# Head pairs recorded five units apart in place of four, with a new table of offsets

## Chip, core and metric

The kernel runs on one core of a Trainium2 chip. The metric is the device time of one execution in microseconds (us); the kernel before takes 849.22 us, the median of three runs (847.69 to 849.58). Engines are called PE (TensorE), DVE (VectorE), ACT (ScalarE), POOL (GpSimd) and SP (SyncE, which issues the DMAs).

## The reference, cut to what matters

Attention over 4 batches and 8 heads of 576 tokens, followed by two networks of two layers each, 512 to 2048 to 512, on 2304 tokens. The attention is the sum of one on means of four tokens and one in which a token sees its neighbours less than four away.

```python
q_d = q.reshape(B, H, Sd, 4, D).mean(axis=3)            # the same for k, v
out_up = np.repeat(sm_attn(q_d, k_d, v_d), 4, axis=2)
scores = np.where(np.abs(pos[:, None] - pos[None, :]) < 4, scale * q @ k.T, -1e9)
out_local = softmax(scores) @ v
x = (out_up + out_local) as 2304 x 512
h = x @ w_in                                            # first network
x = (np.maximum(h, 0.0) + np.log1p(np.exp(-np.abs(h)))) @ w_out
h = x @ w2_in                                           # second network
return (h * np.cos(h)) @ w2_out
```

## The kernel before, in words

Attention is done for a pair of heads at a time: 16 pairs, four to a batch, named p00 to p33 (batch, then pair). The networks go over five tiles of tokens (four of 512, one of 256). A layer's 2048 features are 16 units f of 128. In the names of the operations "L1 t f" is unit f of tile t in the first layer of the first network (matmuls "mm", then abs, relu, exp, ln, and G, gh, gl, which make the float16 parts of the result), "L2 t f d" its second layer (d is a half of the outputs), "L2 t f mm, keep, plus, turns, sin" the first layer of the second network and "L4 t f d" its last. Layer one of tile 0 takes float32 matmuls for its first six units (L1279 on PE; L1288, L1292 and L1296 on ACT; L1300 on DVE, which empties the PSUM buffer h) and float16 ones for the others (L1343, with L1440 to L1452 on ACT and L493 on DVE); the second layer is L1316 (float32) or L1524 (float16); the second network is L1378 and L1574. The four big weights (w1i, w1o, w2i, w2o) arrive compressed in eight blocks each. A block is loaded into one of two staging buffers stg, rebased on ACT (L638), joined on DVE (join1 L482, join2 L646), bounded on ACT (L668), and after a maximum over all partitions (PE L523 "wmax spread", DVE L529 "wmax", two small DVE steps "wfit") split into a high and a low half (L497, L493).

A pair's steps, by letter: A are the scores of the neighbour attention (PE L813, L819), A4 their exponential (ACT L854), B those of the pooled one (PE L912, L919; B1a and B2 are ACT L934 and L939, three instructions), C turns the weights round (PE L974; copies C0 and C1, ACT L503), D the same for the pooled ones (PE L1010, L994; copy D1, ACT L503), E is the product with the values (PE L1080, L1099; output E1, DVE L1123).

A planner sets the order. Each operation has a cost and one engine, or a choice of two (some copies and scalings go to ACT or DVE, whichever is free). A backward pass gives each a due time, on PE in the order in which the operations were recorded. Then `MOVES` adds offsets to these by name ("p13" for a whole pair, "p13 D1#1" for the first operation of that name). A list scheduler takes the operations by due time, puts each engine's instructions in one fixed order, and gives out the buffers: two PSUM buffers h for the first layers during the attention stage (four from about 130 us on), four larger ones ("any"). Where PE would stand idle for long in the first part of the program, the scheduler puts in a zero matmul (L1865, "filler"). So one changed offset can change the order on all engines, and the order of loads on SP.

`POS1`, `POS2` and `POS3` say after how many recorded units of the first network the pairs p10 to p13, p20 to p23 and p30 to p33 are recorded; p00 to p03 stand at the start. On the chip each engine works through its fixed order and waits at semaphores.

Of the kernel before, what the change touches and what calls it, by code (L numbers as in the profile page):

```python
# [23 lines left out]
B, H, S, D = 4, 8, 576, 64  # L24
# [26 lines left out]
POS2 = (37, 41, 45, 49)  # L51
POS3 = (54, 58, 62, 66)
# [355 lines left out]
def build(tc, qk, vw, vd, mask, w1i, w1o, w2i, w2o, out):  # L408
# [3 lines left out]
    with ExitStack() as ctx:  # L412
# [1208 lines left out]
        back = [(1, 0, f) for f in range(F0, NF)]  # L1621
        pos = dict(zip([*POS1, *POS2, *POS3], pairs[4:]))
        at = 0
# [326 lines left out]
```

## Time and profile before

| | |
|---|---|
| runs | 847.69, 849.22, 849.58 us |
| the profiled execution | 849.41 us, of which 847.3 us are the span of its trace |
| PE busy | 98% of the span |
| DVE busy | 85%; 96% from 48 to 100 us |
| ACT busy | 63%; 80% from 48 to 100 us |
| granted TensorE clock | 1.00 in all slices |
| data moved | 59.6 MB, mostly in the first 100 us |

The profile is one execution. A timeline row gives the start and the length of a run of like instructions, "xN" how many, and in brackets the idle time ahead of it with what ended that. PE's ends are modelled and overlap the next start by some tenths, so the distance from start to start is the better length: the 18 matmuls 128x512 in float16 that start at 214.03 us stand 0.22 us apart.

### The profile page before, as it was taken

How to read it: one execution, taken by the hardware profiler on the slowest of the kernel's cores; microseconds unless marked ns; L12 is line 12 of the kernel's file. 1: busy time of each engine (PE TensorE's matmuls, PEld its weight loads, DVE VectorE, ACT ScalarE, POOL GpSimd, SP SyncE). 2: the span in 40 equal slices, each digit the busy share in tenths (PEclk: the TensorE clock that was granted, in tenths of full speed). 3: DMA queues.
4: the chain of work that ended last, by engine and by line, in shares of the span. 5: the costliest groups of instructions: out<-in, count | busy, mean ns of one | idle time of the engine just before them, and what ended most of it. 6: DMA issues, size and time to landing. Idle time of an engine off the chain costs nothing.

```text
span 847.3 us, 15779 instructions
## 1 busy us (share of the span) xinstructions
PE 832.5 (98%) x6342; PEld 493.3 (58%) x6342; DVE 718.0 (85%) x1483; ACT 530.4 (63%) x960; POOL 1.8 (0%) x9
## 2 busy tenths in 40 slices
PE   7999999999999999999999999999999999999998
PEld 3654454555545555444557876666657667567564
DVE  6999999988668865999999989988699889678763
ACT  3568899686356567599989965544265655435431
POOL 0000000000000000000000000000000000000000
PEclk9999999999999999999999999999999999999999
DMA  9888440102210300205214200000000100000010
GB/s 276 274 291 298 164 159 27 59 6 90 62 45 1 117 1 2 67 36 196 100 50 150 101 1 1 1 1 27 26 1 1 51 1 1 24 27 1 1 50 25
DMA packets 14504, 59.57 MB, mean 70 GB/s; under 512 B 1696, under 2 KB 2080, under 8 KB 10336
## 3 DMA queue, kind: packets, MB, share of 16 engines
q1 hardware_dynamic: 14432, 58.58, 20.3%
q8 instruction: 49, 0.80, 0.4%
q14 instruction: 23, 0.19, 0.1%
HBM read 53.85 MB, written 4.72 MB: 69 GB/s over the span
## 4 chain that ended last, share of the span: by engine, by line
PE 83%; DVE 9%; DMA 4%; ACT 3%; issue 1%; POOL 0%; POOLq 0%; DVEq 0%; SPq 0%
PE any L1574 22%; PE any L1524 20%; PE h L1378 19%; PE h L1343 18%; DMA vd<-vd 2%; DMA stg<-w1i 2%; DMA stg<-w1o 1%; PE any L1099 1%; DVE w1i_t L646 1%; DVE sm L485 1%; DVE w1o_t L646 1%; DVE w1i_t L493 1%; PE any L819 1%; DVE vd L485 1%; PE any L974 1%
## 5 line engine op out<-in xcount | busy, mean ns | idle before, releaser
L1574 PE MATMUL any<-w1i_t,g 128*128 128x512 f16 x864 | 198.9, 379 | 1.0 <-DVE w1o_t L499 0.8
L1343 PE MATMUL h<-xt,w1i_t 128*128 128x512 f16 (+1 forms) x888 | 178.0, 356 | 0.1
L1378 PEld LDWEIGHTS <-w2i_t 128*128 128x128 f16 x1536 | 150.3, 98 | 33.8 <-issue 0.9
L1524 PE MATMUL any<-g,w1o_t 128*128 128x512 f16 (+1 forms) x792 | 158.1, 353 | 0.0
L1574 PEld LDWEIGHTS <-g 128*128 128x128 f16 x864 | 84.5, 98 | 87.8 <-issue 1.9
L1343 PEld LDWEIGHTS <-w1i_t 128*128 128x128 f16 x888 | 86.4, 98 | 83.7 <-issue 2.1
L1524 PEld LDWEIGHTS <-w1o_t 128*128 128x128 f16 x888 | 85.5, 98 | 79.4 <-issue 1.2
L485 DVE TENSOR_TENSOR g<-td,g 128x512 f16<-128x512 f32 (+1 forms) x146 | 92.0, 630 | 5.6 <-ACT g L503 2.4
L1378 PE MATMUL h<-xt,w2i_t 128*128 128x256 f16 x720 | 94.8, 273 | 0.7 <-ACT pu L1406 0.7
L1476 ACT ACTIVATE tc<-ta 128x512 f32<-128x512 f32 (+1 forms) x80 | 46.6, 585 | 58.0 <-DVE ta L485 47.9
L1378 PE MATMUL h<-w1o_t,w2i_t 128*128 128x256 f16 x624 | 79.4, 273 | 0.0
L1465 ACT ACTIVATE ta<-hs,quarter,i 128x512 f32<-128x512 f32 x64 | 51.5, 809 | 41.0 <-DVE hs L485 39.0
L503 ACT ACTIVATE g<-td 128x512 f16<-128x512 f32 (+1 forms) x78 | 46.2, 592 | 40.8 <-DVE td L1480 33.0
L1440 ACT ACTIVATE ta<-h,i 128x512 f32<-128x512 f32 (+1 forms) x74 | 47.0, 635 | 24.4 <-PE h L1343 23.5
L485 DVE TENSOR_TENSOR hs<-h,hs 128x512 f32<-128x512 f32 (+1 forms) x96 | 56.5, 598 | 6.3 <-PE h L1378 5.9
L1480 DVE SCALAR_TENSOR_TENSOR td<-hs,r,tc 128x512 f32<-128x512 f32 x64 | 48.0, 749 | 13.3 <-ACT tc L1476 11.8
L1444 ACT ACTIVATE tb<-h,r 128x512 f32<-128x512 f32 (+1 forms) x74 | 47.0, 635 | 15.5 <-PE h L1343 15.5
L493 DVE SCALAR_TENSOR_TENSOR td<-ta,sg,tb 128x512 f32<-128x512 f32 (+1 forms) x64 | 43.8, 684 | 13.2 <-ACT ta L1452 12.5
L485 DVE TENSOR_TENSOR ta<-ta,tb 128x512 f32<-128x512 f32 (+1 forms) x80 | 50.5, 636 | 1.3
L1452 ACT ACTIVATE ta<-ta,one 128x512 f32<-128x512 f32 (+1 forms) x74 | 49.9, 676 | 1.4
L1470 DVE TENSOR_SCALAR tb<-ta 128x512 f32<-128x512 f32 (+1 forms) x80 | 31.6, 398 | 14.8 <-ACT ta L1465 14.5
L1448 ACT ACTIVATE ta<-ta 128x512 f32<-128x512 f32 (+1 forms) x74 | 43.0, 583 | 0.2
(197 smaller groups left out, 1044.5 us busy)
## 6 DMA issues: line engine op xcount, KB each, us to landing
qk<-qk SPq DMA_DIRECT2D x16, 589.0 KB, 7.9
stg<-w1i SPq DMA_DIRECT2D x8, 1024.0 KB, 6.4
stg<-w1o SPq DMA_DIRECT2D x8, 1024.0 KB, 5.0
stg<-w2i SPq DMA_DIRECT2D x8, 1024.0 KB, 6.3
stg<-w2o SPq DMA_DIRECT2D x8, 1024.0 KB, 4.8
vw<-vw SPq DMA_DIRECT2D x16, 320.0 KB, 4.0
out<-w1o_t SPq DMA_DIRECT2D x17, 256.0 KB, 2.0
vd<-vd SPq DMA_DIRECT2D x8, 288.0 KB
```

The lines of the kernel that those rows point to most:

```text
L485: eng[e].tensor_tensor(out=out, in0=in0, in1=in1, op=op)
L493: nc.vector.scalar_tensor_tensor(out=out, in0=raw, scalar=s, in1=other, op0=ALU.mult, op1=op)
L1343: nc.tensor.matmul(h.t[:, 0:n], l, r, start=(i == 0), stop=(i == 11))
L1378: nc.tensor.matmul(h.t[:, a : a + 256], l, r, start=(i == 0), stop=(i == n - 1))
L1440: act(n, 1, True), lambda: nc.scalar.activation(out=a(), in_=h.t[:, 0:n], func=AF.Abs, scale=col(o.i1, f)),
L1444: act(n, 1, True), lambda: nc.scalar.activation(out=b(), in_=h.t[:, 0:n], func=AF.Relu, scale=col(o.r1, f)),
L1452: act(n, 1), lambda: nc.scalar.activation(out=a(), in_=a(), func=AF.Ln, bias=one),
L1465: act(n, 2, psum), lambda: nc.scalar.activation(out=a(), in_=h.t[:, a0 : a0 + n], func=AF.Identity, scale=col(o.i2, f), bias=quarter), [h, ...
L1476: act(n), lambda: nc.scalar.activation(out=r(), in_=a(), func=AF.Sin, scale=TWOPI),
L1480: dve(n, False, 1), lambda: nc.vector.scalar_tensor_tensor(out=td.t[:, 0:n], in0=h.t[:, a0 : a0 + n], scalar=col(o.r1, f), in1=r(), op0=AL ...
L1524: nc.tensor.matmul(a.t[:, i, 0:n], l, r, start=(first and j == 0), stop=(last and j == 2))
L1574: nc.tensor.matmul(a.t[:, i], l, r, start=(f == 0 and j == 0), stop=(f == NF - 1 and j == 2))
```

## The change

The pairs p20 to p33 are recorded five units apart where they were four apart, with p20 one unit later (38 for 37) and p33 seven (73 for 66). The `MOVES` table is another: of its entries nearly all are replaced. Nothing else differs, so what is computed by which matmul is the same. From `before` to `after` the lines of the code move by 11 (L1279 becomes L1290). One filler more is put in (77 for 76), and eight copies or scalings go from ACT to DVE.

```diff
-POS2 = (37, 41, 45, 49)
-POS3 = (54, 58, 62, 66)
+POS2 = (38,43,48,53)
+POS3 = (58,63,68,73)
 MOVES = {
...
-    "L1 0 15": 28.5, "L1 0 15 ln#1": -68, "L1 0 2 abs#1": 262, "L1 0 3": -132, "L1 0 4": -424.5, "L1 0 5": 18.5,
...
+    "L1 0 15": 129, "L1 0 15 mm#1": -13, "L1 0 2": -130.5, "L1 0 4": 48, "L1 0 5": 18.5, "L1 0 6": -45,
...
```

The new table moves instructions from the first microsecond on. Three places follow, each first in the kernel before and then in the changed one.

PE, about 60 us into the program, the first layer's third and fourth unit of tile 0. h_829 and h_830 (h_814 and h_813 after) are the two PSUM buffers, raw_161 to raw_164 the four parts of the input. Before:

```order
L1279 MATMUL h_829<-raw_161,w1i_t 128x512
L1279 MATMUL h_829<-raw_162,w1i_t 128x512
L1279 MATMUL h_829<-raw_163,w1i_t 128x512
L1279 MATMUL h_829<-raw_164,w1i_t 128x512
L912 MATMUL any_89<-qd_119 64x144 x4
L919 MATMUL any_89<-qd_119 32x144 x4
L1279 MATMUL h_830<-raw_161,w1i_t 128x512
L1279 MATMUL h_830<-raw_162,w1i_t 128x512
```

After:

```order
L923 MATMUL any_85<-qd_120 64x144 x4
L930 MATMUL any_85<-qd_120 32x144 x4
L1290 MATMUL h_814<-raw_161,w1i_t 128x512
L1290 MATMUL h_814<-raw_162,w1i_t 128x512
L1290 MATMUL h_814<-raw_163,w1i_t 128x512
L1290 MATMUL h_814<-raw_164,w1i_t 128x512
L1290 MATMUL h_813<-raw_161,w1i_t 128x512
L1290 MATMUL h_813<-raw_162,w1i_t 128x512
```

Before, the scores B of pair p12 stand between the two units (L1 0 4 and L1 0 3); after, the two units (L1 0 5 and L1 0 4) follow each other directly, and the pair's step that stood between them has gone elsewhere.

ACT at the same place, from the ln of unit L1 0 0 to the ln of unit L1 0 1 (ta_94 and ta_95 are the two units' work buffers). Before:

```order
L1296 ACTIVATE ta_94<-ta_94,one 128x512
L638 ACTIVATE w1i_t<-stg_108 128x1024
L668 ACTIVATE w1i_t,bd_w1i<-w1i_t 128x1024
L934 ACTIVATE nd_235<-nd_235 128x3
L497 ACTIVATE up_133<-any_85 128x144
L939 ACTIVATE ed_128,rs_231<-any_89,nd_235 128x144 x3
L1292 ACTIVATE ta_95<-ta_95 128x512
L1296 ACTIVATE ta_95<-ta_95,one 128x512
```

After:

```order
L1307 ACTIVATE ta_94<-ta_94,one 128x512
L1299 ACTIVATE ta_95<-h_813 128x512
L865 ACTIVATE sm_126<-sm_126 128x640
L679 ACTIVATE w1i_t,bd_w1i<-w1i_t 128x1024
L945 ACTIVATE nd_235<-nd_235 128x3
L1303 ACTIVATE ta_95<-ta_95 128x512
L950 ACTIVATE ed_128,rs_231<-any_85,nd_235 128x144 x3
L649 ACTIVATE w1i_t<-stg_109 128x1024
L1307 ACTIVATE ta_95<-ta_95,one 128x512
```

The abs of unit L1 0 1 (L1299) and the exponential of pair p11's scores (L865) now stand between the two logarithms; up (L497) does not.

DVE at the end of the first network, about 482 us into the program, at the maximum of the last two blocks of w2o (L529 on red_261, L540 after). td_98 holds a unit's result, L505 and L485 (L516 and L496 after) make its two float16 parts. Before:

```order
L529 TENSOR_REDUCE red_267<-h_829 128x1
L529 TENSOR_REDUCE red_261<-h_3491 128x2
L493 SCALAR_TENSOR_TENSOR td_98<-ta_94,sg_216,tb_96 128x256
L482 TENSOR_SCALAR s_w2o<-red_261 128x4
L482 TENSOR_SCALAR sx_199<-red_267 128x1
L482 TENSOR_SCALAR s_w2o<-s_w2o 128x4
L529 TENSOR_REDUCE red_269<-h_830 128x1
```

After:

```order
L504 SCALAR_TENSOR_TENSOR td_98<-ta_94,sg_216,tb_96 128x256
L540 TENSOR_REDUCE red_261<-h_3430 128x2
L493 TENSOR_SCALAR c_1_183<-sx_187 128x1
L493 TENSOR_SCALAR s_w2o<-red_261 128x4
L516 CAST g_101<-td_98 128x256
L493 TENSOR_SCALAR s_w2o<-s_w2o 128x4
L496 TENSOR_TENSOR g_101<-td_98,g_101 128x256
```

Before, the maximum stands ahead of the result of unit L1 4 14, which PE takes up four products (L2 4 12 and 13, two halves each) after the spread; after, it stands between the result of unit L1 4 13 and its two float16 parts, and PE takes up that unit (L2 4 13 0) as the next thing after the spread.

## Rows read from the trace of the kernel before

**Rows 1.** The page: busy time and share of the span, instructions by engine.

```profile
PE 832.5 (98%) x6342; PEld 493.3 (58%) x6342; DVE 718.0 (85%) x1483; ACT 530.4 (63%) x960; POOL 1.8 (0%) x9
```

**Rows 2.** Windows: stretch, us, busy time (and instructions) by engine, granted clock, DMA share, GB/s.

```profile
48.00:100.00 52.00, 49.80 (x375) 24.41 (x375) 49.94 (x102) 41.78 (x83) 0.00 (x0) 1.00 0.74 256
100.00:128.00 28.00, 27.89 (x209) 14.24 (x208) 27.72 (x57) 27.73 (x48) 0.00 (x0) 1.00 0.49 163
128.00:215.00 87.00, 87.00 (x715) 43.68 (x714) 79.83 (x164) 67.18 (x121) 0.00 (x0) 1.00 0.16 49
476.00:482.00 6.00, 6.00 (x57) 5.18 (x56) 6.00 (x11) 5.94 (x14) 0.00 (x0) 1.00 0.00 0
```

**Rows 3.** Timeline of PE, 57 to 71 us.

```profile
57.60 0.38 PE L1865 MATMUL any<-zero 128*128 128x512 f16 x1 [0.30 <-ACT aTd L503]
...
60.53 3.70 PE L1279 MATMUL h<-raw,w1i_t 128*128 128x512 f32 x8 [0.29 <-DVE g L1300]
...
65.47 3.70 PE L1279 MATMUL h<-raw,w1i_t 128*128 128x512 f32 x8 [0.45 <-DVE g L1300]
69.75 1.55 PE L1279 MATMUL h<-raw,w1i_t 128*128 128x512 f32 x3 [0.58 <-DVE g L1300]
```

**Rows 4.** Timeline of PE at 86 us.

```profile
86.11 0.38 PE L523 MATMUL h<-ident_s,bd_w1i 128*128 128x128 bf16 x4 [0.38 <-DVE g L1300]
```

**Rows 5.** ACT's groups, 40 to 130 us: count, busy us and mean ns, idle before.

```profile
L638 ACT ACTIVATE w1i_t<-stg 128x1024 f32<-128x1024 f32 x6 | 7.0, 1166 | 4.6 <-DMA stg<-w1i 4.6
L668 ACT ACTIVATE w1i_t<-w1i_t 128x1024 bf16<-128x1024 f32 x8 | 8.6, 1080 | 4.6 <-DVE w1i_t L646 4.6
L1440 ACT ACTIVATE ta<-h,i 128x512 f32<-128x512 f32 x7 | 4.8, 690 | 1.1 <-PE h L1343 0.8 <-DVE td L493 0.2
L939 ACT ACTIVATE ed<-any,nd 128x144 f32<-128x144 f32 x12 | 4.4, 385 | 0.0
L1296 ACT ACTIVATE ta<-ta,one 128x512 f32<-128x512 f32 x6 | 4.3, 723 | 0.1
L1292 ACT ACTIVATE ta<-ta 128x512 f32<-128x512 f32 x6 | 3.8, 632 | 0.0
L1288 ACT ACTIVATE ta<-h 128x512 f32<-128x512 f32 x6 | 3.6, 600 | 0.0
L503 ACT ACTIVATE aTd<-any 72x576 f32<-72x576 f32 x5 | 3.3, 652 | 0.0
L854 ACT ACTIVATE sm<-sm 128x640 f32<-128x640 f32 x4 | 2.9, 757 | 0.0
```

**Rows 6.** Timeline of DVE, 47 to 49 us.

```profile
47.84 0.82 DVE L857 TENSOR_REDUCE rs<-sm 128x10 f32<-128x640 f32 x1 [0.83 <-ACT sm L854]
```

**Rows 7.** Timeline of PE, 214 to 219 us.

```profile
214.03 4.05 PE L1524 MATMUL any<-g,w1o_t 128*128 128x512 f16 x18
218.65 0.58 PE L994 MATMUL any<-ident,ed 128*128 128x128 f32 x3 [0.57 <-DVE sm L485]
```

**Rows 8.** Timeline of all engines at the second network's start, 494 to 498 us.

```profile
495.50 1.28 ACT L1476 ACT_TABLE_LOAD   x1
...
497.74 0.82 PE L1378 MATMUL h<-xt,w2i_t 128*128 128x256 f16 x6 [0.72 <-ACT pu L1406]
```

**Rows 9.** DVE's groups, 462 to 482 us, columns as in rows 5.

```profile
L485 DVE TENSOR_TENSOR g<-td,g 128x256 f16<-128x256 f32 x6 | 2.5, 422 | 0.1
L529 DVE TENSOR_REDUCE red<-h 128x2 f32<-128x256 f32 x3 | 1.3, 420 | 0.0
L505 DVE CAST g<-td 128x256 f16<-128x256 f32 x3 | 0.9, 293 | 0.1
```

**Rows 10.** Timeline of PE at the last change of tile, 812 to 816 us.

```profile
812.86 2.75 PE L1574 MATMUL any<-w1i_t,g 128*128 128x512 f16 x12
815.88 0.81 PE L1574 MATMUL any<-w1i_t,g 128*128 128x512 f16 x3 [0.27 <-DVE w1o_t L499]
```

**Rows 11.** Timeline of PE, the first microseconds.

```profile
2.06 3.60 PE L1865 MATMUL any<-zero 128*128 128x512 f16 x9 [2.06 <-POOL zero L1854]
```

139 rows, old and new, of the table MOVES are left out of this document.

## The prediction

> **What bounds the kernel now.** I read the page first: PE is busy for 98% of the span [rows 1], and from 128 to 215 us it is busy without a gap while DVE and ACT are not [rows 2]. So the time is what PE has to do plus the places where PE waits, and a change that leaves the matmuls as they are can only move those places. I read the windows next, to see what paces the early part: from 48 to 100 us DVE is busy 49.94 of 52 us and PE 49.80 with all waits and fillers in it, and from 100 to 128 us ACT is busy 27.73 of 28 [rows 2]. There PE waits for results of engines that are themselves full. Last I read PE's timeline for the waits one by one, taking lengths from start to start, since ends are modelled. A float32 unit of layer one (8 records of L1279) lasts about 3.6 us when nothing stops it (3.70 in the row, the ends overlapping); the one at 65.47 is followed by the next at 69.75, that is 4.28, of which some 0.65 are the wait for G [rows 3]. Counted so, PE loses 3.5 us between 55 and 95 us: at 57.60, 60.53, 65.47 and 69.75 [rows 3], at 86.11 and just ahead of it [rows 4], and in two of less than 0.2. Behind 100 us it loses little: 0.73 at 218.65, where the D of pair p22 waits for DVE (18 matmuls of 0.22 from 214.03 end at about 217.9) [rows 7]; 0.88 at 497.74, where a PSUM buffer of the second network is emptied late because ACT loads a table for 1.28 us at 495.50 [rows 8]; and 0.41 to 0.43 at each of four changes of tile in the last layer, as at 815.88, which starts 3.02 us after 12 matmuls of 0.216 each began [rows 10]. These 6.8 us (3.5 + 0.73 + 0.88 + 4 x 0.42) and the first 50 us are all that an order can win; nothing sets a floor under what it can lose.
>
> **The change part by part.** All sums go against the profiled execution, 849.41 us, of which the trace spans 847.3; it is 0.2 us above the median of the runs. The loads, weights and matmuls are the same, so no term comes from work, apart from one filler more: +0.22, the step of a matmul of its size [rows 7].
>
> *Units 0 to 5 of tile 0 (about 50 to 70 us).* Layer one of this stage has two PSUM buffers. A unit's matmuls start when the unit two places before has been emptied by G on DVE, and G needs ln on ACT. In the new order L1 0 4 follows L1 0 5 directly, and between the G's that free their buffers ACT has, from ln to ln, abs 0.60, the exponential of p11's scores 0.76, a bound 1.08, B1a 0.21, exp 0.63, three B2 of 0.385, a rebase 1.17 and ln 0.72 [rows 5], 6.3 us by the means and about 5.4 when neighbours overlap by a tenth each. DVE's twelve instructions in the same place come to 4.9. PE has one unit of 3.6 [rows 3]. PE waits the difference: 1.3 by DVE, 2.7 by ACT without overlap, and I take 1.8. Ahead of it L1 0 5 waits for the first G: DVE has 17 instructions since p10's B, 9.3 us by their groups' means, PE 8.5 us of matmuls, and with the way between engines 1.1 (0.6 to 1.5). Behind it p10's D waits for the copy C1, which on ACT stands behind the abs of L1 0 4: 0.60 and two copies of about 0.5 and 0.4, against p10's C and one spread, 0.65 on PE; with the way there and back 0.9 (0.5 to 1.2). The units L1 0 6 and L1 0 8 then cost 0.4 (0 to 0.8). Together 4.2.
>
> *The last early pair (to about 95 us).* PE's p13 E needs the copy D1 on ACT. In the new order ACT has 23 instructions from the relu of L1 0 13 to that copy, of 0.50 to 1.17 each, 18.0 us by their means [rows 5]; PE has two float16 units of 12 matmuls of 0.22, six half-units of the float32 second layer of some 1.75, p13's C and D and a spread, 17.0 up to E. ACT is full there already in the kernel before [rows 2]. I take 0.8 (0 to 1.5; the upper end if the load of w1o's block 5, whose rebase is among the 23, comes late too).
>
> So the early stage loses 5.0 in place of 3.5: **+1.5**, between -1.1 with all lower ends and +4.2 with all upper ones. The cover of these waits is gone where the pair's step between two units has gone; before, p12's B stood there and the wait behind it was still 0.45 [rows 3].
>
> *128 to 460 us.* The wait at 218.65 goes, since p22's D has other work ahead of it: -0.73 [rows 7]. p22's A and E and p32's E now stand nearer to what they wait for (a bank that DVE empties against 1.7 us of PE's work): +0.6 (0 to 1.8), as DVE has free time here [rows 2]. Sum **-0.13**. What is late next is PE itself.
>
> *The change to the second network (470 to 500 us).* The new order goes past the table load with other matmuls in between: -0.88 [rows 8]. In its place PE has the spread of the last two blocks of w2o directly ahead of L2 4 13, and on DVE the maximum stands ahead of that unit's float16 parts. From the end of the spread PE waits for the maximum 0.42, one or two small steps of 0.15, the cast 0.29 [rows 9] and the way there and back, some 0.4: about 1.4, and a little more where the low part (0.42) follows late; I take 1.5. Below it is 0.6, if DVE reads the spread while PE still has matmuls of L2 4 12. Above it is 3.5, since the spread itself needs the bound of w2o's block 6, which now stands behind another rebase, a high half and a bound of more than 1 us each on an ACT that is busy 5.94 of 6 us here [rows 2]. L4 0 0 0 then waits for the low part of L2 0 0: +0.5 (0 to 1.3, one table load). Sum **+1.1**.
>
> *Changes of tile in the last layer (560 to 820 us).* Before, four of them have some 1.3 us of matmuls between the last use of a bank and its next, and wait 0.42; the order after has so little at two only (L4 1 0 1 and L4 4 0 0), and 1.95 or more at the others: **-0.85** [rows 10].
>
> Sum: 0.22 + 1.5 - 0.13 + 1.1 - 0.85 = +1.8, and 849.4 + 1.8 is **851.3 us**.
>
> *The clock.* PE's granted clock is 1.00 in every stretch here [rows 2], also behind the waits of rows 3. [...]
>
> **The rivals.** *The early waits only change place.* DVE and ACT have the same work before p13's E as before and are full [rows 2]; if they set the pace, PE gets to the end of that stage at the same time wherever it waits, and the +1.5 is 0. For it: 49.94 of 52 us on DVE. Against it: PE's waits come from order inside a few us, and DVE's share falls when it waits in turn. With 1.0 to 1.5 at the spread the sum is then -0.2 to +0.3, about 849.5.
>
> *Faster.* DVE waits for the exponential of p10's scores for 0.83 at 47.84 [rows 6], just ahead of the first G. In the new order other work stands there. If DVE and ACT come 1.1 us or more earlier to the G of L1 0 0, then L1 0 5 no longer waits, and the gain passes on to L1 0 4, L1 0 6 and p13's E, all of which wait for these two engines; of 5.0 only p10's D with 0.9 stays. Early stage -2.6, total 849.4 + 0.22 - 2.6 - 0.13 + 1.1 - 0.85 = 847.2. It decides from about 1.1 us on, and 0.83 is short of that; so it is the lesser case.
>
> [...]
>
> *The spread waits for the bound.* The term of 1.5 is then 3.5 and with the upper ends of two others the time is about 855. For it: ACT has next to no free time at 476 to 482 us [rows 2].
>
> **How the numbers follow.** Chances: the sum as it stands 0.50, early waits that only change place 0.27, faster 0.13, the bound 0.06, the clock 0.04. Of the first, whose own spread is about 849.9 to 853.5, I count 0.44 as slower by over 0.2% and 0.06 within it; of the second 0.25 within and 0.02 faster; the third is faster, the last two slower. 0.2% is 1.7 us, about what a measurement of this kernel can tell from no change: slower means above 850.9, faster below 847.5. So slower 0.54, same 0.31, faster 0.15. The range goes from 848.0, which leaves out most of the faster case, to 855.0, which takes in the bound's case.
>
> **What the profile after would show.** PE idle for over 1 us ahead of L1 0 5 and L1 0 4 with G as the releaser; p10's D with ACT's copy; the spread of w2o followed by an idle time of 1.2 to 1.8 us ahead of L1535, released by DVE; no wait at p22's D; two waits at changes of tile in place of four. The prediction is wrong if PE comes to p13's E no later than before against its own work (then the second or the third case holds), if the maximum of w2o hides, or if a wait shows that I saw no cause for, such as a load that comes late because the loads' order on SP is another.

## The result, and the profile after

The changed kernel takes 853.77 us (four runs, 853.31 to 854.21), the kernel before 848.46 (four runs, 846.03 to 849.58): the ratio is 1.0068, with a 95% interval from 1.0047 to 1.0089. That is slower by more than 0.2%. Its profiled execution took 854.17 us and spans 852.3, before 849.41 and 847.3: 5.0 us more in the span where the prediction's sum had 1.8. The direction and the range held; the size did not.

The page's busy times after, which answer to [rows 1]:

```profile
PE 837.2 (98%) x6343; PEld 494.9 (58%) x6343; DVE 721.1 (85%) x1491; ACT 521.9 (61%) x952; POOL 1.8 (0%) x9
```

PE does one matmul more (the filler). Its busy time is 4.7 us longer all the same, and slower matmuls are one reason: the windows after, with columns as in [rows 2], show a stretch at a lower clock.

```profile
48.00:100.00 52.00, 47.23 (x364) 23.54 (x364) 46.40 (x96) 43.93 (x85) 0.00 (x0) 0.93 0.58 190
56.00:60.00 4.00, 1.15 (x17) 0.44 (x17) 2.85 (x5) 4.00 (x7) 0.00 (x0) 0.83 0.90 264
60.00:64.00 4.00, 4.00 (x5) 1.82 (x6) 4.00 (x11) 4.00 (x12) 0.00 (x0) 0.50 0.98 314
64.00:68.00 4.00, 4.00 (x9) 1.65 (x8) 2.73 (x5) 1.76 (x4) 0.00 (x0) 0.81 0.34 135
100.00:128.00 28.00, 27.72 (x164) 13.31 (x162) 28.00 (x50) 27.55 (x52) 0.00 (x0) 1.00 0.68 240
```

From 48 to 100 us PE is busy 2.57 us less than before and DVE 3.54 less, and the granted clock, 1.00 before, is 0.93, with 0.50 from 60 to 64 us. From 100 to 128 us PE's busy time is within 0.2 us of that before.

To see where the 5.0 us went, I followed PE's steps in order and took from the start of each the sum of all PE work ahead of it, every kind with its own step from start to start. What is left is the time that PE has lost by then:

| PE has lost, us | before | after | difference | predicted |
|---|---|---|---|---|
| up to 48 us | 7.05 | 5.79 | -1.3 | none |
| from there to p13's E (123.72 before, 130.66 after) | 4.45 | 10.05 | +5.6 | +1.5 |
| from there to 460 us | 2.73 | 2.48 | -0.25 | -0.13 |
| change to the second network | 1.07 | 2.50 | +1.4 | +1.1 |
| from there to the end | 1.87 | 1.14 | -0.73 | -0.85 |
| one filler more | | | +0.22 | +0.22 |

The rows add up to the 5.0 us. The terms behind p13's E came out within 0.3 us of the prediction. The early stage alone cost +4.3 (-1.3 and +5.6) where I had +1.5. Its first row need not come from the order: in nine traces of the change and of kernels made from it by later edits, whose instructions are the same up to there, the first matmul of layer one starts between 44.97 us (e7_more) and 47.67 us (e6_end2), in the change at 45.27. So single traces are best compared from that matmul on. The timeline of all engines after shows how it begins, at the place of [rows 3]:

```profile
56.00 1.12 ACT L649 ACTIVATE w1i_t<-stg 128x1024 f32<-128x1024 f32 x1 [2.90 <-DMA stg<-w1i]
...
57.15 0.69 DVE L493 TENSOR_SCALAR w1i_t<-w1i_t 128x1024 int32<-128x1024 int32 x1 [3.12 <-ACT w1i_t L649]
57.76 0.42 DVE L496 TENSOR_TENSOR sm<-any,nm 128x256 f32<-128x256 f32 x1
...
58.05 0.71 ACT L1307 ACTIVATE ta<-ta,one 128x512 f32<-128x512 f32 x1
...
58.23 0.48 PE L923 MATMUL any<-qd 64*64 64x144 f32 x8 [2.82 <-DVE sm L496]
```

Block 5 of w1i is loaded from 47.45 us, when its staging buffer comes free, and lands at 55.98. ACT has its rebase (L649) next in its order and stands still 2.90 us for it; the ln of L1 0 0 (L1307) is queued behind. DVE has the block's join1 (L493) next and stands still 3.12 us; the second half of p11's A3 (L496) is queued behind that, and PE's B of p11 needs it. All three engines wait for one load. PE's part of the sequel, up to L1 0 2 (75.58 us after, 69.75 before):

```profile
59.97 9.86 PE L1290 MATMUL h<-raw,w1i_t 128*128 128x512 f32 x16 [0.62 <-DVE g L1311]
69.66 0.71 PE L985 MATMUL any<-ident,sm 128*128 128x128 f32 x5
...
71.22 0.85 PE L1021 MATMUL any<-ident,ed 128*72 128x128 f32 x6 [0.80 <-ACT aT L514]
72.06 0.59 PE L1876 MATMUL h<-zero 128*128 128x512 f16 x2
73.05 0.40 PE L534 MATMUL h<-ident_s,bd_w1i 128*128 128x128 bf16 x4 [0.40 <-ACT w1i_t L679]
73.58 0.59 PE L1876 MATMUL any<-zero 128*128 128x512 f16 x2
```

L1 0 5 and L1 0 4 stand in the first row. No idle time shows between them, yet the sixteen matmuls last 9.7 us, to the start of the next row, in place of 7.2: L1 0 5 ran at a granted clock of 0.56 on average (0.50 up to 64 us) and took 6.26 us in place of 3.6. PE is not seen waiting for the G of L1 0 1 there, since it is slow instead of idle: that G ends at 64.97, 1.4 us behind the point where a unit at 1.00 would have ended (59.97 and 3.6), and L1 0 4 starts at 66.23, so 1.26 us of the slow unit came through. The next G on DVE then stands still 1.51 us for the ln of the slow unit:

```profile
64.28 0.69 DVE L1311 SCALAR_TENSOR_TENSOR g<-h,ta 128x512 f32<-128x512 f32 x1 [0.23 <-ACT ta L1307]
...
68.47 0.69 DVE L1311 SCALAR_TENSOR_TENSOR g<-h,ta 128x512 f32<-128x512 f32 x1 [1.51 <-ACT ta L1307]
```

DVE's share is the key to what follows. The windows from zero to the start of L1 0 2, before and after; PE has done 60.2 and 60.7 us of work by then, so the two points compare:

```profile
0.00:69.75 69.75, 61.98 (x843) 35.39 (x844) 60.31 (x117) 38.46 (x96) 1.77 (x9) 1.00 0.86 283
```

```profile
0.00:75.58 75.58, 67.22 (x879) 37.65 (x879) 63.56 (x124) 42.99 (x102) 1.77 (x9) 0.95 0.80 268
```

PE comes there 5.83 us later. DVE was busy 3.25 us more ahead of that point (63.56 and 60.31), and not busy 2.58 more (12.02 and 9.44). Of the 2.58, 0.35 are a longer wait for the first load (2.34 in place of 2.00) and 2.23 are what is left of the waits for block 5 (3.12) and behind the slow unit (1.51), less smaller waits that went. In three more traces with the same early order (e4_end, r_after, e6_end2) the 12.02 are 10.74, 11.26 and 13.48. The 3.25 are other work that the new table puts ahead of L1 0 2. By the durations of single instructions they are the two joins of one more block of w1i, 1.90; two more maxima and four of the small steps behind them, 1.64; a G, 0.69; steps for the scale of the next tile, 0.73; against them p10's output E1 and one A3 moved behind, -1.6. That the two differences add up to the 5.83 is so by construction; whether PE follows DVE here is what the experiments had to show.

Late in the program the timeline of PE after shows what stands in place of [rows 8] and [rows 10]:

```profile
486.62 0.29 PE L534 MATMUL h<-ident_s,bd_w2o 128*128 128x128 bf16 x2
487.87 0.27 PE L1535 MATMUL any<-g,w1o_t 128*128 128x256 f16 x1 [0.97 <-DVE g L516]
488.33 1.36 PE L1535 MATMUL any<-g,w1o_t 128*128 128x256 f16 x11 [0.19 <-DVE g L496]
...
598.37 1.46 PE L1585 MATMUL any<-w1i_t,g 128*128 128x512 f16 x6 [0.25 <-DVE w1o_t L510]
...
819.58 0.81 PE L1585 MATMUL any<-w1i_t,g 128*128 128x512 f16 x3 [0.27 <-DVE w1o_t L510]
```

Directly behind the spread of w2o PE waits for the float16 parts of L1 4 13, the cast (L516) first and the low part (L496) after it: 1.15 and 0.35 from start to start, and 0.44 ahead and behind. The wait for the table load has gone. Two changes of tile wait in place of four.

### The profile page after: what moved, and what is told of

Read it like the earlier page. It is cut to its first block, busy times and chain, and to the rows that moved or that the text cites. A ratio compares the mean times of both kernels' runs of the same rounds, so it can differ in the third digit from the quotient of the medians.

```text
span 852.3 us, 15790 instructions
## 1 busy us (share of the span) xinstructions
PE 837.2 (98%) x6343; PEld 494.9 (58%) x6343; DVE 721.1 (85%) x1491; ACT 521.9 (61%) x952; POOL 1.8 (0%) x9
## 4 chain that ended last, share of the span: by engine, by line
PE 82%; DVE 10%; ACT 4%; DMA 2%; issue 2%; SPq 0%; POOL 0%; POOLq 0%; ACTq 0%; DVEq 0%
PE any L1585 22%; PE h L1389 19%; PE any L1535 17%; PE h L1354 16%; PE any L1110 2%; DVE w1i_t L657 1%; PE any L1876 1%; DVE td L504 1%; DMA vd<-vd 1%; DVE w1i_t L504 1%; DMA stg<-w1i 1%; PE any L985 1%; DVE w1o_t L657 1%; PE h L1290 1%; PE any L830 1%
## 5 line engine op out<-in xcount | busy, mean ns | idle before, releaser
L1354 PE MATMUL h<-xt,w1i_t 128*128 128x512 f16 (+1 forms) x888 | 179.2, 356 | 0.3 <-ACT ta L1451 0.3
L1354 PEld LDWEIGHTS <-w1i_t 128*128 128x128 f16 x888 | 86.4, 98 | 83.6 <-issue 2.8
L496 DVE TENSOR_TENSOR g<-td,g 128x512 f16<-128x512 f32 (+1 forms) x146 | 91.9, 630 | 6.2 <-ACT g L514 3.2
L496 DVE TENSOR_TENSOR hs<-h,hs 128x512 f32<-128x512 f32 (+1 forms) x96 | 56.9, 598 | 4.7 <-PE h L1389 4.0
L496 DVE TENSOR_TENSOR ta<-ta,tb 128x512 f32<-128x512 f32 (+1 forms) x80 | 50.6, 636 | 1.4
```

The costliest lines, as they stand in the source:

```text
L496: eng[e].tensor_tensor(out=out, in0=in0, in1=in1, op=op)
L1354: nc.tensor.matmul(h.t[:, 0:n], l, r, start=(i == 0), stop=(i == 11))
```

## The experiments

Two theories stood against each other. *The load*: block 5 comes late, holds ACT and DVE, and through them PE and its clock; undo that and most of the early loss is gone. *The pace of DVE*: DVE has more to do ahead of the same point of PE's work; PE's waits are where that shows, and one that is taken away comes back at the next place. All kernels below but the last two leave the planner alone and put single operations elsewhere in its finished order, by a function `later`: the first operation of a pair goes directly behind the second. "#2" is the second operation of a name.

### The load's work moved behind the scores (e1_load)

```diff
         ops, all4 = P.order(), list(BANK.tiles)
+        later(ops, [
+            ("w1i5 rebase", "p11 A4"), ("w1i5 join1", "p11 A5"), ("w1i5 join2", "w1i5 join1"),
+            ("w1i5 bound", "p11 B2"), ("w1i3 load", "w1i5 join2"), ("w1i1 rebase", "L1 0 1 ln"),
+        ])
```

> The changed kernel, with the rebase of w1i's block 5 moved behind the ln and abs of units L1 0 0 and L1 0 1 and the exponential of p11 on ACT, its two joins behind p11's second A3, G and A5 on DVE, its bound behind p11's B2, and the rebase of block 1 behind the ln of L1 0 1. Theory 1 (the load of block 5 lands at 55.98 us, and ACT and DVE, which meet it too early in their fixed orders, hold up p11's B and L1 0 5): the idle 2.8 us of PE at 55.4 goes, with it the lower clock (0.50 at 60 to 64 us goes to 1.00), and the time falls by 4.5 to 5.5 us, to about 848.8. Rival (the loads themselves set the pace, so the wait moves to the next block's rebase and to L1 0 4): PE idles for 1.5 to 3 us there instead and the time falls by 0 to 2.5 us.

853.07 us, ratio 1.0045 (1.0030 to 1.0059), against 1.0068 (1.0047 to 1.0089) of the change itself: no more than a trend. The timeline of PE and the window to L1 0 2:

```profile
57.50 3.70 PE L1290 MATMUL h<-raw,w1i_t 128*128 128x512 f32 x8
...
64.62 3.70 PE L1290 MATMUL h<-raw,w1i_t 128*128 128x512 f32 x8 [3.42 <-DVE g L1311]
```

```profile
0.00:73.53 73.53, 63.78 (x879) 35.85 (x879) 63.76 (x124) 43.01 (x102) 1.78 (x9) 1.00 0.83 276
```

The waits at p11's B and at L1 0 5 are gone, and the clock stays at 1.00. But L1 0 4 now waits 3.42 us for G. L1 0 2 starts 2.05 us earlier than in the change, and DVE's time without work ahead of it is 9.77 in place of 12.02: 2.25 less. Counted from the first matmul of layer one, to which this execution came 1.37 us later than the change's, the gain is larger: 26.89 us to L1 0 2, of which DVE is without work for 1.88, where the four traces of the change's early order have 28.91 to 30.31 and 4.01 to 5.41. So the moves took 2.0 to 3.4 us off this stretch. The medians show 0.7 of it, and their intervals, of more than 1 us each way, cannot tell how much reaches the end.

### One join moved (e2_join)

```diff
+        later(ops, [("w1i5 join1", "p11 A3#2")])
```

> The changed kernel with one instruction moved: join1 of w1i's block 5 stands behind p11's second A3 on DVE; ACT's order is left. Theory 1 (ACT's rebase, which waits for the load, is ahead of the ln that G needs): p11's B starts at 55.4 us in place of 58.2, but L1 0 5 starts at 60.0 as before, so the idle 2.8 us move from p11's B to L1 0 5, and the time stays within 0.7 us of the changed kernel. Rival (the bank that p11's B waits for, held by DVE alone, is the cause): the time falls by 2.8 to 5.5 us.

853.43 us, 1.0054 (1.0032 to 1.0077). PE's timeline:

```profile
56.87 0.48 PE L923 MATMUL any<-qd 64*64 64x144 f32 x8
...
59.88 3.70 PE L1290 MATMUL h<-raw,w1i_t 128*128 128x512 f32 x8 [2.16 <-DVE g L1311]
...
65.39 1.12 PE L1290 MATMUL h<-raw,w1i_t 128*128 128x512 f32 x2 [1.81 <-DVE g L1311]
```

B of p11 no longer waits, and the clock stays at 1.00; but L1 0 5 starts at 59.88 as in the change (59.97), because its G needs the ln that ACT has queued behind the rebase. The join on DVE was one of two queues behind the load, and the one on ACT alone is enough to hold PE. Here ACT waited 1.49 us for the block, and the stretch from the first matmul of layer one to L1 0 2 took 27.29 us, 0.40 more than in e1_load.

### PE kept busy through the wait (e3_fill)

```diff
+        # zero matmuls 128x192 into unused columns, ahead of p11's B
+        ops[at0:at0] = [Op(-1, pe(0.08), warm, (), "fill") for _ in range(22)]
```

> The changed kernel with 22 zero matmuls of 192 columns put into PE's order ahead of p11's B, where PE stands idle for 2.8 us; nothing else moves. If the lower clock that follows the idle time makes L1 0 5 slow (6.26 us from its start to that of L1 0 4, in place of 3.6): the granted clock stays 1.00 at 60 to 64 us, L1 0 5 lasts 3.6 us, and the time falls by about 2.7 us, to 851.1, although the wait itself stays. If that unit is slow for another reason (its buffer, the transfers beside it), or the fillers do not keep the clock: no change, 853.8.

854.48 us, 1.0053 (1.0027 to 1.0079). PE's timeline and a window:

```profile
57.58 1.98 PE L1889 MATMUL any<-zero 128*128 128x192 f16 x22
...
60.27 3.70 PE L1290 MATMUL h<-raw,w1i_t 128*128 128x512 f32 x8
...
67.62 5.40 PE L1290 MATMUL h<-raw,w1i_t 128*128 128x512 f32 x8 [3.64 <-DVE g L1311]
```

```profile
68.00:72.00 4.00, 4.00 (x7) 1.55 (x6) 3.93 (x7) 1.86 (x2) 0.00 (x0) 0.57 0.03 13
```

L1 0 5 ran at 1.00 (60 to 64 us) and took 3.70 us by its row, not 6.26. L1 0 4 then waited 3.64 us for its buffer, and the clock fell behind that wait instead, to 0.57. This is no test of the clock's price, though, since the loads came otherwise in this execution: block 5 landed 4.93 us after its issue (8.53 in the change), ahead of ACT's rebase, and block 1 after 9.47 us, so that ACT stood still for that one, with the ln of L1 0 1 behind it:

```profile
65.11 1.12 ACT L649 ACTIVATE w1i_t<-stg 128x1024 f32<-128x1024 f32 x1 [2.25 <-DMA stg<-w1i]
```

So L1 0 4's buffer came late by a load of its own.

### The unit behind the maximum of w2o, earlier (e4_end, e6_end2)

```diff
+        later(ops, [("L1 4 13 G", "w2o6 join2"), ("L1 4 13 gh", "L1 4 13 G"), ("L1 4 13 gl", "L1 4 13 gh")])
```

> The changed kernel with the result of L1 4 13 and its two float16 parts put ahead of those of L1 4 14 on DVE, so that the maximum of w2o no longer stands between the spread and what PE takes up next. The prediction's step (PE waits 1.15 + 0.35 us behind the spread for the maximum and the cast): these waits go, -1.3 to -1.9 us, to about 852.2. Rival (the spread's own wait for the bound of block 6, or L1 4 14's parts, come next): the wait moves behind by two half-units and -0.6 us or less is left.

855.82 us, 1.0081 (1.0058 to 1.0104). PE's timeline, with a row of DVE's behind it:

```profile
485.67 2.78 PE L1535 MATMUL any<-g,w1o_t 128*128 128x256 f16 x24
...
489.28 0.27 PE L1535 MATMUL any<-g,w1o_t 128*128 128x256 f16 x1 [0.82 <-ACT g L514]
...
490.80 1.36 PE L1535 MATMUL any<-g,w1o_t 128*128 128x256 f16 x11 [1.25 <-DVE g L496]
```

```profile
489.04 1.28 DVE L504 SCALAR_TENSOR_TENSOR w1i_t<-w1i_t,s_w2o 128x1024 f16<-128x1024 f32 x1
```

The waits at L2 4 13 are gone (24 matmuls without a break), and come back two units on, where the low part of L1 4 15 stands on DVE behind the low half of a block of w2o, 1.28 us. By the starts of the same matmuls, 0.67 us more is lost here than in the change. e6_end2 went one step further and moved that low half too:

```diff
+            ("w2o5 low", "L1 4 15 gl"), ("w2o6 high", "w2o5 low"), ("xhi#21", "L1 4 15 ln"),
```

> The changed kernel with e4_end's edit (result of L1 4 13 ahead of that of L1 4 14), and in addition the two long instructions that held up L1 4 15 there put behind: w2o's low half of block 5 behind the low part of L1 4 15 on DVE (with the high half of block 6 behind it), and a scaling of 0.7 us behind the ln of L1 4 15 on ACT. e4_end's waits of 0.99 and 1.41 us at L2 4 15 should fall to 0.3 to 0.6 together, and those at L2 4 13 stay away: against the changed kernel -1.3 to -1.7 us from 480 to 492 us, about 852.3. Rival (DVE is full up to 490 us and only the place of the wait can be chosen): 1.5 us or more are lost again at L2 0 0 or L4 0 0.

855.84 us, 1.0082 (1.0057 to 1.0107). PE's timeline:

```profile
492.01 0.27 PE L1535 MATMUL any<-g,w1o_t 128*128 128x256 f16 x1 [0.36 <-ACT g L514]
...
500.50 0.82 PE L1389 MATMUL h<-xt,w2i_t 128*128 128x256 f16 x6 [1.42 <-DVE hs L496]
```

L2 4 15 waits 0.36 now, and the second network's third unit 1.42, for DVE again; 0.68 us more is lost than in the change. That fits a sum of waits that is set by what DVE has to do, while the order says who waits, but no run took work off DVE there. Both medians lie some 2 us above the change's; the rest of that is left open.

### The change again (r_after)

> The changed kernel once more, beside the others on the same chip, to see how far its early waits vary from one execution to the next: the waits at p11's B (2.98), L1 0 5 (0.95), the slow unit (2.82) and p13's E (0.37) were read from one trace. If they come from the order, they stand within 0.5 us of these; if the loads' landing decides, the wait at p11's B varies by 1 us or more with the landing of block 5 of w1i, and the lower clock comes and goes with it. Time 853 to 855 in both cases.

853.15 us, 1.0056 (1.0039 to 1.0073). The waits are the same ones within 0.4 us (p11's B 2.64 in place of 2.98, then 0.95, p10's D 0.96, late 1.15 and 0.35), but for the slow unit L1 0 5, which took 5.24 us in place of 6.26, with the granted clock 0.63 in place of 0.50 from 60 to 64 us. So 1 us of that unit's delay belongs to the one execution. e6_end2, whose early order is the same, shows that the waits themselves go by when the load lands: it came to layer one 2.40 us later than the change, block 5 landed at 56.88, PE stood idle 1.34 us at p11's B, L1 0 5 ran at 1.00, and L1 0 4 waited 2.40 us and was the slow one (0.86 from 64 to 68 us, 0.71 from 68 to 72). The stretch to L1 0 2 took 29.64 us all the same.

### A pair's step put back between the two units (e5_p10)

```diff
+        later(ops, [  # besides the moves of e1_load
+            ("p10 A5", "p11 A5"), ("p10 N1", "p10 A5"), ("p10 N2", "p10 N1"), ("p10 A6", "p10 N2"), ("p10 B4", "p10 A6"),
+            ("p10 C", "p11 B2"), ("p10 C0", "p10 C"), ("p10 C1", "p10 C0"), ("p10 D", "p10 C1"), ("L1 0 1 ln", "p10 D"), ("p10 D1", "L1 0 1 ln"),
...
+            ("p10 E", "p10 D1"),
```

This puts p10's weights (A5 to B4 on DVE), its C and D with their copies, and its E between L1 0 5 and L1 0 4, where the kernel before has a pair's step. It also puts the ln of L1 0 1 behind p10's D.

> The changed kernel with block 5's rebase and joins moved behind as in the run before (e1_load), and in addition p10's last steps earlier: on DVE A5, N1, N2, A6 and B4 of p10 directly behind p11's A5, on PE p10's C, D and E between L1 0 5 and L1 0 4, their copies on ACT accordingly. Theory 2 (DVE and ACT set when G of L1 0 1 comes, at about 64 us in both kernels; the kernel before has p10's C, D and E to do on PE by then, the changed one has not): the wait of 3.7 us at L1 0 4 that e1_load showed falls to 0.5 to 1.2, the wait of 0.96 at p10's D goes or shrinks, and the time falls by 2.5 to 3.5 us against e1_load, to about 850. Rival (DVE alone is the pace up to p13's E, wherever PE waits): the waits come back at L1 0 2, L1 0 3 or at the spread behind them, and the time stays within 1 us of e1_load.

853.47 us, 1.0055 (1.0038 to 1.0072). PE's timeline and the window to L1 0 2:

```profile
65.67 3.70 PE L1290 MATMUL h<-raw,w1i_t 128*128 128x512 f32 x8 [0.35 <-DVE g L1311]
...
71.48 0.59 PE L1876 MATMUL h<-zero 128*128 128x512 f16 x2 [2.06 <-DVE red L540]
```

```profile
0.00:73.94 73.94, 65.08 (x878) 36.45 (x878) 63.10 (x121) 42.96 (x101) 1.77 (x9) 0.99 0.81 268
```

L1 0 4 waits 0.35 in place of e1_load's 3.42. In its place p10's D waits 0.86, its E 0.73, and PE 2.06 for the maximum of w1i on DVE, and L1 0 2 starts at 73.94 where e1_load had 73.53. Three us of waiting moved and nothing was won. DVE had 0.66 us less to do ahead of L1 0 2 than in e1_load and stood still 1.07 us more, so the run shows that waits move, and not by itself which engine sets the pace. Behind the 2.06 us the clock fell to 0.50, and L1 0 2 took 5.93 us in place of 3.53:

```profile
72.00:76.00 4.00, 3.59 (x10) 1.58 (x10) 4.00 (x12) 2.93 (x7) 0.00 (x0) 0.50 0.95 326
```

### More work on DVE (e7_more)

```diff
+        # besides the moves of e1_load: p11 A5, the sum of a pair's rows, done three times
+        for _ in range(2):
...
+            ops.insert(ops.index(a5) + 1, again)
```

> e1_load's kernel with p11's A5 done three times over on DVE in place of once: 1.6 us more work for DVE (0.81 each) in front of block 5's joins, nothing else. Theory 2 (up to about 75 us DVE sets the pace: in the changed kernel and in its variants so far L1 0 2 starts at 68.2 to 68.4 us plus DVE's idle time before it): L1 0 2 and everything behind start 1.6 us later than in e1_load at equal idle time, and the time rises by 1.3 to 1.7 us. Rival (loads or ACT set it, DVE has slack inside that stretch): idle time of DVE shrinks by as much, and the time stays within 0.4 us of e1_load.

855.14 us, 1.0066 (1.0045 to 1.0087), 2.1 us above e1_load by the medians, with intervals that overlap. The stretch from the first matmul of layer one to the start of L1 0 4, in e1_load and then here, holds the whole edit:

```profile
46.64:64.62 17.98, 14.56 (x146) 6.37 (x145) 16.41 (x34) 13.05 (x31) 0.00 (x0) 1.00 0.90 298
44.97:64.42 19.45, 14.56 (x146) 6.37 (x145) 17.96 (x36) 13.05 (x31) 0.00 (x0) 0.96 0.81 273
```

PE and ACT do the same in both, DVE has 1.55 us more to do, its time without work stays (1.57 and 1.49), and L1 0 4 comes 1.47 us later. So the two extra sums came through almost whole: DVE had no slack here that could have hidden them. The window to L1 0 2, which starts 2.13 later than e1_load's:

```profile
0.00:75.66 75.66, 65.60 (x879) 36.62 (x879) 65.54 (x127) 43.10 (x102) 1.77 (x9) 0.95 0.81 274
```

That the 2.13 are near the added work is luck. This execution came to layer one 1.67 us earlier than e1_load's, and behind the longer wait L1 0 4 ran at 0.50 (64 to 68 us) and 0.80 (68 to 72), for which DVE stood still 2.06 us at the maximum behind it:

```profile
64.42 6.25 PE L1290 MATMUL h<-raw,w1i_t 128*128 128x512 f32 x8 [4.89 <-DVE g L1311]
```

```profile
71.31 0.29 DVE L540 TENSOR_REDUCE red<-h 128x1 f32<-128x128 f32 x1 [2.06 <-PE h L534]
```

With e1_load that decides for the pace of DVE up to L1 0 4, its waits included. The load's part, with the clock's fall behind it, is the 2.0 to 3.4 us that e1_load took off the stretch; with both gone L1 0 2 still starts 3.78 us later than before, and 3.25 us of work put ahead on DVE are of that size. That these cost what they last is concluded from adding to them; an order with five units between the pairs that puts less on DVE there was not made.

### The kernel before, mended at the same places (e8_early, e9_best)

If DVE paces the stage, the kernel before should gain where DVE stands still in it: behind 40 us that is mostly for ACT's rebases and for the exponential of [rows 6]. e8_early takes the kernel before and moves eight operations there; e9_best adds five late ones, which give p22's D and the changes of tile of [rows 7] and [rows 10] more of PE's work in between.

```diff
+        later(ops, [  # e8_early, on the kernel before
+            ("p10 A5", "w1i2 join2"), ("w1i6 join1", "p11 A6"), ("L1 0 5 exp", "L1 0 5 abs"), ("L1 0 5 ln", "L1 0 5 exp"),
+            ("p12 B4", "p12 A6"), ("w1o1 join1", "L1 0 5 G"), ("w1o1 join2", "w1o1 join1"), ("w1o6 load", "w1o1 join2"),
+            # e9_best also
+            ("p22 D", "L2 1 4 1"), ("L4 1 0 1", "L2 1 2 mm#3"), ("L4 1 0 0", "L4 1 2 1"),
+            ("L4 3 0 0", "L2 4 7 mm"), ("L4 4 0 0", "L2 4 10 mm"),
+        ])
```

> The kernel before with DVE's three idle places of the early stage filled by work that is ready: p10's A5 behind join2 of w1i's block 2 (0.83 idle at 47.8 us), join1 of block 6 behind p11's A6 (0.65 at 66.1), join1 and 2 of w1o's block 1 behind p12's B4 and the G of L1 0 5, with exp and ln of L1 0 5 ahead of that block's rebase on ACT (0.91 at 82.9). Theory 2: DVE's idle time up to L1 0 9 falls by 1.5 to 2.4 us, PE's waits at L1 0 3, L1 0 2 and at the two spreads (0.5, 0.8, 0.5, 0.5) fall by that, and the time by 1.2 to 2.2 us, to about 846.8. Rival (the waits of the kernel before are local, as I had priced them, and the loads set the rest): only the two spreads' waits go, -0.3 to -1.0.

> e8_early's kernel, and in addition five places of PE's order behind 200 us turned: p22's D behind the half-unit L2 1 4 1 that follows it, and the first product of a new tile (L4 1 0 1, L4 1 0 0, L4 3 0 0, L4 4 0 0) behind the matmuls that follow it, so that 0.65 to 1.3 us more of PE's work stand between a bank's last use and its next. If PE's waits there (0.73 and four of 0.42) are local, since DVE and ACT have free time behind 128 us: -2.0 to -2.4 us against e8_early, to about 844.6, and the kernel beats both. Rival (the matmuls moved ahead wait for their own buffers or inputs): half of it or less.

e8_early: 847.81 us, 0.9993 (0.9975 to 1.0012), no difference that its twelve runs can show. e9_best: 845.56 us (seven runs, 844.39 to 846.53), 0.9959 (0.9942 to 0.9976), faster than both kernels. Its window to L1 0 2, and what DVE waits for from 40 to 97 us (the totals, the times, the longest):

```profile
0.00:67.65 67.65, 61.75 (x844) 35.41 (x844) 60.59 (x117) 39.20 (x96) 1.77 (x9) 1.00 0.86 292
```

```profile
DVE red L529 <- PE h L523: 0.6, 1, 0.6
DVE nm L845 <- PE any L819: 0.3, 1, 0.3
```

DVE no longer waits for ACT in the early stage, its time without work to L1 0 2 is 7.06 (before 9.44), and PE reaches that unit 2.10 us earlier. Counted as above, e9_best's execution lost 0.8 less than before up to 48 us, where no edit acts, 2.1 less from there to 130 us, and 1.3 less behind that (the changes of tile 0.91 in place of 1.69, with a new wait at 736.18 us among the 0.91, and p22 0.36 in place of 0.73). e8_early's execution lost 1.0 more than before up to 48 us, and 0.7 less from there to 130, so the early edits, the same in both, gave 0.7 in one execution and 2.1 in the other. How much of the 3.1 us they carry is not settled by these runs; that the thirteen edits together gain is.

### Both spacings without their offsets (e10_none4, e11_none5)

What of the result is the spacing, and what the table? Both kernels with an empty table:

```diff
-MOVES = {
...
+MOVES = {}
```

> The kernel before with an empty table of offsets: pairs four units apart, the planner's own order. Without offsets I expect more waits than with either table, 855 to 875 us. It is the base for the run beside it (e11_none5), which has the pairs five units apart and no offsets either.

> The changed kernel with an empty table of offsets: pairs five units apart, the planner's own order. The pairs that are recorded further apart start behind 128 us, where DVE and ACT have free time in both kernels. If the spacing itself costs or gains little and the change's loss comes from the new table's order of the first 75 us: within 2 us of e10_none4, and up to 100 us the two orders lose PE about the same. If wider spacing is what costs: slower than e10_none4 by 4 us or more; if it helps and the table hid it: faster by 2 us or more.

Spacing of four without offsets: 871.55 us, 1.0283 (1.0247 to 1.0320). Spacing of five without offsets: 906.51 us, 1.0680 (1.0655 to 1.0705). I had expected the two within 2 us of each other; they are 35 apart, and not in the early stage. The windows of the two from 360 to 480 us, and for the second the largest wait of PE there and the window around it (L1277 in this shorter file is L1354 of the changed kernel, the first layer's float16 matmul):

```profile
360.00:480.00 120.00, 119.17 (x659) 63.74 (x657) 92.00 (x200) 86.60 (x150) 0.00 (x0) 1.00 0.14 47
```

```profile
360.00:480.00 120.00, 94.82 (x421) 41.68 (x420) 81.99 (x163) 69.89 (x98) 0.00 (x0) 0.87 0.15 53
380.00:400.00 20.00, 2.83 (x16) 1.30 (x15) 19.52 (x43) 11.35 (x10) 0.00 (x0) 0.69 0.37 130
```

```profile
PE h L1277 <- DVE sx L416: 16.9, 1, 16.9
```

PE waits 16.9 us in one place for the scale of the next tile, on a DVE that is busy 19.52 of 20 us with what stands ahead of it: DVE's order paces PE here too. The fitted table takes all of this back (up to 460 us the change loses 0.25 less than before behind p13's E). So the result is that of the two tables more than of the spacings. The old table with the new spacing, or the other way round, was not tried.

## Why the prediction was right or wrong

*What bounds the kernel.* That the time is PE's work plus its waits, and that the matmuls stay, held: the differences of the table add up to the span. That DVE is full in the early stage was read rightly too. The mistake is in what I did with it: I sized each PE wait by the order within a few us, and left DVE's fullness to a rival.

*Units 0 to 5 of tile 0* is the step that failed, with +1.5 in the sum for the early stage and +4.3 measured. Two of its waits were sized well: L1 0 5 0.95 (1.1 predicted) and p10's D 0.96 (0.9). At L1 0 4 the agreement is luck: it came 1.7 us late in r_after (1.8 predicted), but because L1 0 5 was slow and not because PE waited for G. Three things were missing. The wait of 2.98 at p11's B, from a load that is issued when a buffer comes free and lands 8.5 us later: I named such a load as a sign of being wrong in my last paragraph, and did not follow its block to the instructions that stand first in line for it. The fall of the granted clock behind it, to 0.50. And 1.03 us at fillers and spreads, of which 0.40 are seen as a wait for the bound of w1i on ACT. With the first two gone (e1_load) the stretch to L1 0 2 is 2.0 to 3.4 us shorter, and L1 0 2 still starts 3.78 us later than before. What I should have sized is DVE: 3.25 us more of its instructions stand ahead of L1 0 2 in the new order, which can be counted from the order at the durations of the trace before, and its waits for the load and behind the slow unit, 2.2 us net, come on top.

*The last early pair*: 0.37 in place of 0.8, and from L1 0 2 to p13's E the change lost 0.9 less than before. That fits DVE's pace as well: work that was done ahead of L1 0 2 need not be done behind it. Of the 5.2 us that PE had lost more than before at L1 0 2, 4.3 remained.

*128 to 460 us*, *the second network*, *the last layer*: -0.25 for -0.13, +1.4 for +1.1, -0.73 for -0.85. The wait at p22's D and the one for the table load went as said, p22's A (0.14) came as said, 0.41 came at p32's A where I had named its E, and the two changes of tile that I named are the two that wait. At the second network 1.15, 0.35 and 0.44 stand for 1.5, which is low by 0.4. The ways between the engines, 0.4 in it and 0.3 in the 1.1 at L1 0 5, came from no row, and no run shows these figures; in the change 0.09 us lie between the spread's end and the maximum, 0.04 between the cast's end and PE, and 0.05 between the end of the G of L1 0 0 and L1 0 5. A wait of 0.41 came in the second network's first layer (at 503.34 us), where the sum had 0.5 at L4 0 0 0, which did not wait.

*The rivals.* "The early waits only change place" had the mechanism: e5_p10 and e6_end2 show waits of 1.4 to 3.4 us that move and do not shrink. But it took DVE's work before p13's E as the same and so its price as nil. It forgot that the pace goes by what stands ahead of each point, and that a full engine can also be made to wait (DVE 3.12 us for block 5). "Faster" did not come: it needed the G of L1 0 0 1.1 us earlier or more, and it starts at 59.23 in place of 59.80, with ACT and DVE held by the load. The clock, to which I had given 0.04, did fall, from 1.00 to 0.50 behind a wait of 2.82 us, longer than any in the trace of before, where the longest took 2.06. The 0.04 was my estimate, with no fall of the clock in the trace of before to work it out from. The price of the fall in the change is not the 2.7 us by which the unit is longer, since PE would have waited 1.4 us for G there: 1.26 us came through to L1 0 4, and DVE stood still 1.51 us at the next G (0.50 in r_after). "The spread waits for the bound" did not come.

## What to carry to other kernels

Where an engine other than PE is as full as DVE here (49.94 of 52 us [rows 2]), size a new order by that engine: add up its instructions ahead of a fixed point of PE's work, and its own waits, in both orders. Here PE followed (1.55 us more of DVE's work brought L1 0 4 1.47 later in e7_more), and waits that were taken away singly came back a little later (3.42 us at L1 0 4 in e1_load). Compare two traces from an instruction just ahead of the edit: executions of the same instructions came to such a point up to 2.7 us apart. For every load that changes place, look up when its buffer comes free and what stands behind its first reader on each engine (here ACT's 2.90 us and DVE's 3.12). And a table of offsets fitted to one spacing says nothing of the spacing itself: without tables the two were 35 us apart, in a part of the program where the fitted kernels differ by 0.25 us.

## What the runs showed of the hardware

The granted clock of TensorE fell after waits of 2.06 us (e5_p10, to 0.50), 2.40 (e6_end2, 0.71 from 68 to 72 us), 2.64 (r_after, 0.63 from 60 to 64), 2.82 (the change, to 0.50), 3.64 (e3_fill, 0.57 from 68 to 72) and 4.89 (e7_more, to 0.50), and stayed at 1.00 after 3.42 us (e1_load) and after 2.16 and 1.81 close together (e2_join). So the length of the last wait alone does not tell in these runs, and what else counts is left open. A float32 unit of eight matmuls took 6.26 us from start to start at 0.56 on average (the change), 6.25 by its row at 0.50 and then 0.80 (e7_more), and 3.53 from start to start at 1.00 (e5_p10). What a slow unit cost hung on what waited for it: 1.26 us of the 2.7 at the next unit in the change, where PE would have waited anyway, and 2.06 us of DVE's time in e7_more.

One and the same load, block 5 of w1i, landed 4.93 us (e3_fill) to 8.53 us (the change) after its issue in the nine traces. In six of them it landed between 55.60 and 56.29 us, whether issued at 47.45 or at 48.98, so an execution that came to it earlier waited longer: ACT stood still 2.90 us in the change and 1.49 in e2_join, which came to layer one 1.52 us later.
